# Staging the 64-bit words of one piece of weights in the place of the x of later chunks

## The chip, the core and the metric

The kernel runs on one core of one Trainium2 chip. The metric is the device time of one execution in microseconds (us). An execution ends when the last output row has been written to memory. The kernel before was timed three times: 731.48, 734.87 and 738.36 us, median 734.87 us.

## What is computed

Two stages follow one another. The first is a linear recurrence (RWKV-7) over 768 time steps with a 40x40 state for each of 4 batches and 8 heads. Its outputs, one row of 320 numbers for each of 3072 tokens, go through a feed-forward layer of width 2048.

```python
for t in range(S):                      # S = 768; state is (B, H, D, D) = (4, 8, 40, 40)
    y[:, :, t] = einsum('bhd,bhde->bhe', rt, state)
    Sa = einsum('bhde,bhe->bhd', state, at)
    state = state * wt[:, :, None, :] - einsum('bhd,bhe->bhde', Sa, bt) + einsum('bhd,bhe->bhde', vt, kt)
x = y.transpose(0, 2, 1, 3).reshape(3072, 320)
h = x @ w_in                            # 320 -> 2048
out = (h / (1 + exp(-1.702 * h))) @ w_out   # 2048 -> 320
```

The inputs are float32, but w_in and w_out are 64-bit floats. The kernel turns them into float32 on the chip.

## The kernel before

**Chunks and units.** Time is cut into 12 chunks of 64 steps. A chunk has two units (two batches each), so there are 24 units. `prep`, `inverse` and `solve` are the recurrence of one unit. `inverse` is a chain of five levels: a group of matmuls (`ps_level`), a subtraction on DVE (`E`, L686), a 32x32 transpose on DVE (`ES`, L648), a spreading to twice the size on POOL, DVE or ACT (`EX`, L653 and L655), and the next level. The copy `W` (L684) runs beside it. `solve` ends with the matmuls `ps_y`, with `zr` (L837) and with the product `x` (L847). `part_with` writes that x to memory (`x_dram`, L857), and `get_back` reads it back turned (`xT`, L861).

**The feed-forward layer.** `mlp(c)` takes the xT of both units of chunk c. `ps_up` multiplies by w_in in four groups (q = 0 to 3) of 40 matmul calls, ACT applies the gelu to each group (`g`, L882), and `ps_down` multiplies by w_out in two passes (p = 0 and 1) of eight parts (m = 0 to 7), eight matmul calls each. Each call of a float32 matmul appears as two matmuls in the trace. xT has three slots. Chunk c uses slot c mod 3, so chunk 0 uses slot 0, chunk 1 slot 1 and chunk 2 slot 2.

**The weights.** They come in eight pieces of 128x1280 64-bit words (1280 KB each). Pieces 0 to 3 are w_in, and `ps_up` group q needs piece q. Pieces 4 to 7 are w_out: parts m = 0 and 1 of `ps_down` need piece 4, parts 2 and 3 piece 5, parts 4 and 5 piece 6, and parts 6 and 7 piece 7. `weight(n, ...)` plans six steps for a piece: the transfer into a staging place (L433), one ACT instruction (`rebased`, L413), and five DVE instructions: L417, L421 and L422, L425, and L429 (`joined`). L429 writes the finished float32 words into `w_sb`. A staging place is twice the size of a finished piece. The list `raws` (L399) says where each piece is staged: a positive number is a position in the part of `w_sb` that is not yet filled, and -4 and -2 are the two halves of the buffer `extra`, called A and B here. In the kernel before, pieces 0, 4 and 6 use A one after the other, and pieces 3, 5 and 7 use B. Pieces 1 and 2 lie in `w_sb`. A transfer waits until the piece before it in the same place is joined (`before`, L407).

**What sets the order.** The class `Plan` writes the program out. Every step is a task with a rank, costs on the engines that may run it, and the tasks it needs. `order()` walks through time with these costs, and for each free engine takes the able task of the lowest rank. `paced()` repeats this in four rounds with release times for the feed-forward layer, and keeps the plan that ends first by its own costs. The tasks are then issued in that order, so each engine runs its instructions in a fixed order. The transfers are all issued by SP, in one order. A weight's rank is one of `RANKS` (L243: 14 to 41), a recurrence step's about 10 times its unit, and a feed-forward matmul's 10000 and more.

Of the kernel before, what the change touches and what calls it, by code (L numbers as in the profile page):

```python
# [21 lines left out]
INT64 = mybir.dt.int64  # L22
# [203 lines left out]
def rwkv7_gelu_quick(ctx: ExitStack, tc: tile.TileContext, time_d, v_d, w_d, wc_d, ak_d, b_d, rv_d, w_in, w_out, out):  # L226
    nc = tc.nc
    H, D, S = 8, 40, out.shape[0] // 4
    DM = H * D
# [3 lines left out]
    PIECE = w_in.shape[2]  # L233
    NF = w_in.shape[0] * PIECE // DM
    NM = NF // 2
    NK = DM // 64
# [17 lines left out]
    plan = Plan(dict(logw=3, wc=3, G=1, wch=3, wz=2, time=2, ak=2, b=2, rv=2, FT=3, GT=1, kh=2, bh=2, zr=2, rz=2,  # L254
                     A=1, B=1, RV=2, E0=2, W0=2, P21=2, W=2, E=2, ES=2, EX=2, T=2, Tc=1, QT=1, zraw=2, zT=1, M=2, x=1, xT=3, g=4, ob=1), 4)
    tiles, psums, drams = {}, {}, {}

    def single(name, shape):
        return const.tile(shape, FP32, tag=name, name=name)

    def buf(name, n, shape, dt=FP32):

        if (name, n) not in tiles:
            s = n % plan.slots[name]
            tiles[name, n] = work.tile(shape, dt, tag=f"{name}{s}", name=name)
        return tiles[name, n]
# [20 lines left out]
    def act(n):  # L287
        return {"ACT": 210.0 + 0.76 * n}
# [39 lines left out]
    for p in HALF:  # L328
        q = slice(p.start, p.start + MID)
# [59 lines left out]
    w_sb = single("w_sb", [128, NK * NM * 128 + NF * DM])  # L389
    w_in_sb = w_sb[:, :NK * NM * 128].rearrange("p (m k f) -> p m k f", m=NM, k=NK)  # L390
    w_out_sb = w_sb[:, NK * NM * 128:]

    extra = single("extra", [128, 4 * PIECE])


    most, least = (float(np.array(x, np.uint32).view(np.float32)) for x in (0x0FEFFFFF, 0x9FEFFFFF))


    raws = [-4, 4, 6, -2, -4, -2, -4, -2]  # L399

    def weight(n, rank, src):
        at = raws[n]
        raw = lambda: (w_sb[:, at * PIECE:(at + 2) * PIECE] if at > 0 else extra[:, (at + 4) * PIECE:(at + 6) * PIECE]).bitcast(INT64)

        scale = lambda: w_sb[:, n * PIECE:(n + 1) * PIECE].bitcast(INT32)

        before = [("weight", m) for m in range(n) if raws[m] == at]  # L407
        there = [("weight", m) for m in range(n) if raws[m] in (n, n - 1)]
        word = lambda dt, w: raw().bitcast(dt).rearrange("p (n two) -> p n two", two=2)[:, :, w]

        def rebased(t):

            nc.scalar.activation(scale().bitcast(FP32), word(FP32, 1), ACT.Prelu, scale=2.0 ** -112, alpha=2.0 ** 32)  # L413

        def bounded(t):

            nc.vector.tensor_scalar(scale().bitcast(FP32), scale().bitcast(FP32), least, most, ALU.max, ALU.min)  # L417

        def exponent(t):

            nc.vector.tensor_scalar(word(INT32, 1), scale(), 3, -2 ** 23, ALU.logical_shift_left, ALU.bitwise_and)  # L421
            nc.vector.tensor_single_scalar(scale(), scale(), 3, op=ALU.logical_shift_left)  # L422

        def fraction(t):
            nc.vector.scalar_tensor_tensor(word(FP32, 1), in0=word(UINT32, 0), scalar=2.0 ** -52, in1=word(FP32, 1),  # L425
                                           op0=ALU.mult, op1=ALU.mult)

        def joined(t):
            nc.vector.tensor_add(scale().bitcast(FP32), scale().bitcast(FP32), word(FP32, 1))  # L429

        one, two = 170.0 + 0.48 * PIECE, 150.0 + 1.05 * PIECE
        T = lambda *names: [(name, n) for name in names]
        plan.add(rank, {"SP": 350.0}, lambda t: nc.sync.dma_start(raw(), src), reads=before, writes=T("wt"), size=128 * PIECE * 8)  # L433
        plan.add(rank, act(PIECE), rebased, reads=T("wt") + there, writes=T("rebased"))
        plan.add(rank, {"DVE": one, "sbuf": True}, bounded, reads=T("rebased"), writes=T("bounded"))
        plan.add(rank, {"DVE": 2 * one, "sbuf": True}, exponent, reads=T("bounded"), writes=T("exponent"))
        plan.add(rank, {"DVE": two, "sbuf": True}, fraction, reads=T("exponent"), writes=T("fraction"))
        plan.add(rank, {"DVE": two, "sbuf": True}, joined, reads=T("fraction"), writes=T("weight"))

    def weights():  # L440
        for n in range(len(raws)):
            weight(n, RANKS[n], w_in[n] if n < NQ else w_out[n - NQ])
# [116 lines left out]
    at = lambda tiles, n: tiles[n % len(tiles)]  # L559
# [1 line left out]
    both = lambda i: zr_of(i)[:, :8 * 104].rearrange("p (j n) -> p j n", n=104)  # L561
    zraw_of = lambda i: buf("zraw", i, [128, 8, D])
    M_of = lambda i: buf("M", i, [128, 8, 104])
    xT_of = lambda c: buf("xT", c, [128, 2, NK, 128])
    kh_of, bh_of = lambda i: kh_t[i % 2], lambda i: bh_t[i % 2]
    zT_of = lambda i: zT_t[i % plan.slots["zT"]]

# [165 lines left out]
    def solve(i):  # L733
        c, p = divmod(i, 2)
        R = 20 * (i // 2) + 5 * (i % 2)
        T = lambda *names: [(n, i) for n in names]
        ahT = lambda: ak_of(i)[:, 0]

        if c > 0:
            plan.add(R, {"DVE": 490.0, "sbuf": True}, lambda t: nc.vector.tensor_mul(  # L740
                both(i)[:, :, 64:], zraw_of(i - 2), wz_of(i).unsqueeze(2).to_broadcast([128, 8, D])),
                     reads=[("zraw", i - 2), ("wz", i)], writes=T("zr"))
# [12 lines left out]
            def read_state(t):  # L755

                ps, rT = psum(t, "ps_rz"), rv_of(i)[:, 0]
                for u, b in product(BITS, BITS):
                    for f, e in QUARTERS:
# [5 lines left out]
                     reads=T("zT"), writes=T("rz"), pair=("rz", i))  # L765
# [94 lines left out]
            for h in HALF:  # L860
                nc.sync.dma_start(xT_of(c)[h, p].rearrange("q k n -> q (k n)"), drams[i].rearrange("(q k) n -> q (k n)", q=64))  # L861
        plan.add(-50, {"SP": 700.0}, part_with, reads=T("x"), writes=T("xd"), size=DM * 512)
        plan.add(-50, {"SP": 700.0}, get_back, reads=T("xd"), writes=[("xT", c), ("xs", (c, p))], size=2 * DM * 512)


    g_of = lambda n: buf("g", n, [128, 2, 2, 256])
# [60 lines left out]
    for i in range(NU):  # L927
        decay(i)
        if i + 3 < NU:
            load_w(i + 3)  # L930
        if i + 2 < NU:
            logarithm(i + 2)
        if i >= 2:
            load(i)
        prep(i)
        inverse(i)
        solve(i)
        if i % 2:
            mlp(i // 2)
# [88 lines left out]
```

## Time and profile before

| What | Value |
|---|---|
| median of three runs | 734.87 us |
| the profiled execution's own time | 741.96 us |
| its span, first to last instruction | 740.3 us |
| PE busy | 679.0 us (92%) |
| DVE busy | 445.9 us (60%) |
| ACT busy | 343.8 us (46%) |
| POOL busy | 214.5 us (29%) |
| mean granted TensorE clock | 0.959 |

PE is TensorE and PEld its loading of weights, DVE is VectorE, ACT is ScalarE, POOL is GpSimd, and SP the engine that issues the transfers. A line of a view of waits has the waiting engine and instruction, then `<-`, then what ended the wait, and then the total in us, the number of waits and the longest one. A line of a timeline has the start and the duration in us, the engine, the line of the code and the tiles (out `<-` in); a bracket at its end is the engine's idle time ahead of it and what ended that. A line of a table of windows has the stretch in us, the busy time of each engine with the number of its instructions, the granted clock of TensorE (1.00 is full), the busy share of the transfer engines and the GB/s that they moved.

### The profile page before, as it was taken

How to read it: one execution, taken by the hardware profiler on the slowest of the kernel's cores; microseconds unless marked ns; L12 is line 12 of the kernel's file. 1: busy time of each engine (PE TensorE's matmuls, PEld its weight loads, DVE VectorE, ACT ScalarE, POOL GpSimd, SP SyncE). 2: the span in 40 equal slices, each digit the busy share in tenths (PEclk: the TensorE clock that was granted, in tenths of full speed). 3: DMA queues.
4: the chain of work that ended last, by engine and by line, in shares of the span. 5: the costliest groups of instructions: out<-in, count | busy, mean ns of one | idle time of the engine just before them, and what ended most of it. 6: DMA issues, size and time to landing. Idle time of an engine off the chain costs nothing.

```text
span 740.3 us, 43272 instructions
## 1 busy us (share of the span) xinstructions
PE 679.0 (92%) x20096; PEld 560.7 (76%) x20096; DVE 445.9 (60%) x795; ACT 343.8 (46%) x666; POOL 214.5 (29%) x279
## 2 busy tenths in 40 slices
PE   4575895899999999999999999999999999999997
PEld 3465773687888977887887888988888798777564
DVE  5788798878558566666557467656666546542000
ACT  4555465445535535545645526445446345332120
POOL 7236124243323333322322233422441421200000
PEclk9576699899999999999999999999999999999999
DMA  7951544243251242341332233341331230110000
GB/s 227 350 177 53 168 139 148 65 117 107 57 169 47 77 122 73 87 136 49 99 102 71 74 95 104 98 120 55 99 101 50 83 93 4 40 48 29 13 9 19
DMA packets 31860, 69.80 MB, mean 94 GB/s; under 512 B 5056, under 2 KB 14272, under 8 KB 30656
## 3 DMA queue, kind: packets, MB, share of 16 engines
q1 hardware_dynamic: 31680, 67.03, 30.1%
q8 instruction: 158, 2.59, 1.5%
q14 instruction: 22, 0.18, 0.1%
HBM read 59.15 MB, written 7.86 MB: 91 GB/s over the span
## 4 chain that ended last, share of the span: by engine, by line
PE 77%; DVE 7%; ACT 5%; DMA 5%; issue 2%; POOL 2%; SPq 2%; DVEq 0%; POOLq 0%; ACTq 0%
PE ps_down L274 25%; PE ps_up L274 25%; PE ps_level L274 7%; PE ps_y L274 4%; PE ps_B L274 4%; PE ps_X L274 2%; PE ps_T L274 2%; PE ps_Q L274 2%; DMA ak<-in_ak 1%; PE ps_rz L274 1%; DVE ES L648 1%; PE ps_N L274 1%; PE ps_RV L274 1%; PE ps_A L274 1%; DMA extra<-in_w_out 1%
## 5 line engine op out<-in xcount | busy, mean ns | idle before, releaser
L274 PE MATMUL ps_up<-xT,w_sb 64*64 64x256 f32 x3840 | 251.3, 379 | 2.7 <-DVE RV L605 1.5
L274 PE MATMUL ps_down<-w_sb,g 64*64 64x320 f32 x3072 | 246.6, 436 | 4.9 <-DVE w_sb L429 2.5
L274 PEld LDWEIGHTS ps_up<-xT,w_sb 64*64 64x64 f32 x3840 | 152.7, 134 | 32.0 <-DVE RV L605 1.6
L274 PEld LDWEIGHTS ps_down<-w_sb,g 64*64 64x64 f32 x3072 | 135.6, 135 | 50.3 <-issue 7.6
L274 PEld LDWEIGHTS ps_level<-W,EX 64*64 64x64 f32 x3840 | 85.3, 141 | 41.6 <-ACT EX L653 14.3
L274 PE MATMUL ps_level<-W,EX 64*64 64x64 f32 (+1 forms) x3840 | 87.4, 226 | 26.6 <-ACT EX L653 11.6
L653 ACT ACTIVATE EX<-ES,quads 128x256 f32<-128x256 f32 x120 | 54.5, 501 | 59.7 <-DVE ES L648 57.5
L684 ACT COPY W<-ps_level 128x512 f32<-128x512 f32 x67 | 39.3, 586 | 71.5 <-PE ps_level L274 71.2
L882 ACT ACTIVATE g<-ps_up 128x1024 f32<-128x1024 f32 x48 | 49.1, 1024 | 42.5 <-PE ps_up L274 42.2
L686 DVE TENSOR_TENSOR E<-two,ps_level 128x256 f32<-128x256 f32 x96 | 39.7, 413 | 48.1 <-ACT W L684 48.0
L655 POOL TENSOR_TENSOR EX<-ES,quads 128x512 f32<-128x512 f32 x26 | 37.7, 1449 | 80.3 <-DVE ES L648 57.6
L648 DVE STREAM_TRANSPOSE ES<-E 128x256 f32<-128x256 f32 x120 | 53.2, 444 | 5.6
L582 POOL TENSOR_TENSOR kh<-time,G 128x320 f32<-128x320 f32 x22 | 19.7, 894 | 123.9 <-PE ps_y L274 72.1
L908 DVE TENSOR_TENSOR ob<-ob,ps_down 128x320 f32<-128x320 f32 x24 | 11.6, 485 | 63.4 <-ACT ob L906 63.0
L785 ACT COPY B<-ps_B 128x416 f32<-128x416 f32 x41 | 20.6, 507 | 62.4 <-PE ps_B L274 62.4
L847 POOL TENSOR_TENSOR x<-zr,FT 128x128 f32<-128x128 f32 x80 | 42.7, 563 | 5.4 <-DVE zr L837 3.4
L643 POOL TENSOR_TENSOR W<-two,E 128x256 f32<-128x256 f32 x22 | 16.1, 731 | 95.5 <-DVE E L637 95.5
L274 PE MATMUL ps_y<-M,bh 64*64 64x104 f32 x768 | 36.7, 253 | 0.6 <-issue 0.6
L274 PE MATMUL ps_y<-RV,kh 64*64 64x104 f32 x768 | 36.2, 254 | 0.3 <-DVE M L801 0.3
L574 POOL TENSOR_TENSOR ak<-ak,FT 128x512 f32<-128x512 f32 x18 | 26.9, 1496 | 26.2 <-DMA ak<-in_ak 20.9
L801 DVE TENSOR_TENSOR M<-ps_X,later 128x832 f32<-128x832 f32 x24 | 24.5, 1019 | 15.9 <-PE ps_X L274 15.9
L655 POOL TENSOR_TENSOR T<-ES,quads 128x512 f32<-128x512 f32 x10 | 12.8, 1278 | 71.1 <-DVE ES L648 66.4
(128 smaller groups left out, 1088.2 us busy)
## 6 DMA issues: line engine op xcount, KB each, us to landing
ak<-in_ak SPq DMA_DIRECT2D x48, 160.0 KB
time<-in_time SPq DMA_DIRECT2D x24, 320.0 KB
rv<-in_rv SPq DMA_DIRECT2D x48, 160.0 KB
xT<-x_dram SPq DMA_DIRECT2D x48, 160.0 KB
wc<-in_wc SPq DMA_DIRECT2D x20, 264.0 KB
extra<-in_w_out SPq DMA_DIRECT2D x4, 1280.0 KB
logw<-in_w SPq DMA_DIRECT2D x24, 160.0 KB
b<-in_b SPq DMA_DIRECT2D x48, 80.0 KB
```

Source lines behind the costliest of these rows:

```text
L274: nc.tensor.matmul(o, lhsT, rhs, start=start, stop=True, skip_group_check=True)
L574: plan.add(R, {"DVE": 690.0, "POOL": 1270.0, "sbuf": True}, lambda t: of(t.engine).tensor_mul(ahT(), ahT(), FT_of(i)), reads=T("ak", "FT") ...
L582: plan.add(R + 4, {"POOL": 870.0, "DVE": 490.0, "sbuf": True}, lambda t, n=n, dst=dst: of(t.engine).tensor_mul(dst(i)[:, :, :D], by_head(t ...
L648: plan.add(rank, dve(256), lambda t: nc.vector.transpose(ES(n), source(t)), writes=[key("ES", n, 6)], **reads)
L653: nc.scalar.activation(dst[:, :, h], ES(n), ACT.Copy, scale=quads[:, h, :1])
L655: of(t.engine).tensor_mul(dst, ES(n).unsqueeze(2).to_broadcast([128, 8, 2, 32]), quads.unsqueeze(1).to_broadcast([128, 8, 2, 32]))
L684: plan.add(rank, any2(512), lambda t: copy(t.engine)(tiles_of(W(n + 1)), blocks(psum(t, ""), 64)), writes=[key("W", n + 1, 5)], pair=pair)
L686: plan.add(rank, dve(256), lambda t: nc.vector.tensor_sub(tiles_of(E(n + 1)), every(two32, [128, 2, 4, 32]), blocks(psum(t, ""), 64)[:, :, ...
L785: plan.add(R, any2(416), lambda t: copy(t.engine)(dst(), psum(t, "")[:, :, :208]), writes=[("Bv", i)] if x and c > 0 else T("B"), pair=(na ...
L801: plan.add(R + 1, dve(832), lambda t: nc.vector.tensor_tensor(M_of(i).rearrange("p (j b) n -> p b j n", b=2), psum(t, "")[:, :, :416].rear ...
L847: of(t.engine).tensor_mul(x[:, b ^ u, b], both(i)[:, at, :64], FT_of(i)[:, at])
L882: plan.add(-45, act(1024), lambda t: nc.scalar.activation(g_of(c * NQ + q).rearrange("p m r n -> p r m n"), psum(t, "").rearrange("p r (m ...
```

## The change

Piece 4 gets a staging place of its own: slots 1 and 2 of xT, which together are exactly as large as one piece of 64-bit words and first hold x for chunks 1 and 2. Piece 5 then follows piece 0 in A (it followed piece 3 in B), piece 6 follows piece 3 in B (it followed piece 4 in A), and piece 7 follows piece 5, now in A. The three slots of xT become one tile, `xT_all`, so that two of them can be addressed as one place. The reading back of x for chunks 1 and 2 additionally waits until piece 4 is joined. No arithmetic is added or taken away. Below L393 the lines move down by six in the changed file; line numbers in the text are those of the kernel before.

```diff
     extra = single("extra", [128, 4 * PIECE])
+    xT_all = single("xT_all", [128, plan.slots["xT"], 2 * NK * 128])
...
-    raws = [-4, 4, 6, -2, -4, -2, -4, -2]
+    spots = {"a": (extra, 0), "b": (extra, 2), "w4": (w_sb, 4), "w6": (w_sb, 6)}
+    raws = ["a", "w4", "w6", "b", "x", "a", "b", "a"]

     def weight(n, rank, src):
         at = raws[n]
-        raw = lambda: (w_sb[:, at * PIECE:(at + 2) * PIECE] if at > 0 else extra[:, (at + 4) * PIECE:(at + 6) * PIECE]).bitcast(INT64)
+        def raw():
+            if at == "x":
+                return xT_all[:, 1:].rearrange("p s n -> p (s n)").bitcast(INT64)
+            tile, k = spots[at]
+            return tile[:, k * PIECE:(k + 2) * PIECE].bitcast(INT64)
...
         before = [("weight", m) for m in range(n) if raws[m] == at]
-        there = [("weight", m) for m in range(n) if raws[m] in (n, n - 1)]
+        there = [("weight", m) for m in range(n) if raws[m] in (f"w{n}", f"w{n - 1}")]
...
-    xT_of = lambda c: buf("xT", c, [128, 2, NK, 128])
+    xT_of = lambda c: xT_all[:, c % 3].rearrange("p (q k n) -> p q k n", q=2, n=128)
...
-        plan.add(-50, {"SP": 700.0}, get_back, reads=T("xd"), writes=[("xT", c), ("xs", (c, p))], size=2 * DM * 512)
+        plan.add(-50, {"SP": 700.0}, get_back, reads=T("xd") + ([("weight", raws.index("x"))] if c in (1, 2) else []), writes=[("xT", c), ("xs", (c, p))], size=2 * DM * 512)
```

## The prediction, made before the changed kernel was run

> **What bounds the kernel now.** I read the page first, then a table of windows, the chain of work that ended last, the waits between 105 and 150 us, and the timelines of SP, ACT, DVE and PE around them.
>
> ```profile
> PE   4575895899999999999999999999999999999997
> PEclk9576699899999999999999999999999999999999
> ```
>
> These slices of 18.5 us say that PE is full from about 170 us on and has holes before. (In the last slice the final eviction and store are left.) A table of windows puts numbers to it:
>
> ```profile
> 0.00:81.30 81.30, 46.81 (x1512) 42.16 (x1512) 61.48 (x99) 43.45 (x110) 37.06 (x69) 0.71 0.60 199
> 81.30:111.20 29.90, 28.82 (x811) 23.34 (x814) 25.32 (x36) 17.73 (x25) 7.13 (x7) 0.94 0.46 149
> 111.20:144.10 32.90, 21.99 (x646) 15.55 (x638) 27.38 (x39) 17.62 (x36) 9.49 (x8) 0.84 0.31 103
> 144.10:171.60 27.50, 25.37 (x768) 21.73 (x768) 21.13 (x37) 14.45 (x27) 14.00 (x16) 1.00 0.46 129
> 171.60:735.50 563.90, 556.03 (x16368) 457.89 (x16368) 310.08 (x587) 250.14 (x467) 146.82 (x181) 1.00 0.26 75
> ```
>
> From 171.6 to 735.5 PE is busy 556.0 of 563.9 us at full clock. A change in the order of weights can't shorten that, but whatever brings PE earlier to 171.6 moves the end with it. The hole nearest to the change is 111.2 to 144.1: 10.9 us idle, at a clock of 0.84, while DVE is busy 27.4 of 32.9. Its waits:
>
> ```profile
> ACT w_sb L413 <- DMA extra<-in_w_out: 7.0, 1, 7.0
> PE ps_level L274 <- ACT EX L653: 4.9, 2, 4.4
> PE ps_down L274 <- DVE w_sb L429: 2.5, 2, 2.3
> DVE w_sb L417 <- ACT w_sb L413: 1.9, 1, 1.9
> DVE E L686 <- ACT W L684: 1.4, 1, 1.4
> ```
>
> ACT sits 7.0 us in front of the rebasing of a piece whose words have not landed. Queued behind it are a gelu and the EX and W copies, so PE waits 4.4 us for EX and DVE 1.9 and 1.4. SP and the chain say which pieces these are:
>
> ```profile
> 81.25 0.35 SPq L433 DMA_DIRECT2D extra<-in_w_out  x1
> 107.66 0.42 SPq L433 DMA_DIRECT2D extra<-in_w_out  x1
> 112.50 0.35 SPq L433 DMA_DIRECT2D extra<-in_w_out  x1
> ```
>
> ```profile
> 107.66 8.34 DMA extra<-in_w_out
> ...
> 127.65 2.48 DVE extra L425
> 130.16 1.50 DVE w_sb L429
> ...
> 131.70 4.54 PE ps_down L274 x32
> ...
> 142.57 1.48 DVE w_sb L429
> ```
>
> These are pieces 5, 6 and 7; piece 4 was issued at 40.17. Piece 6 could not start until piece 4 had left A (joined at 103.8), landed at 116.0 and was joined at 131.7. Piece 7 was issued when piece 5 left B (112.48), and DVE reached it only behind piece 6: joined at 144.04, with parts 6 and 7 of ps_down from 144.09.
>
> [...] Piece 6 took 8.34, sharing the engines with piece 7. [...] L422 took 1.95 us at 122.70, beside a POOL product, and 0.83 usually. [...] Here 32 ps_down matmuls took 4.54 us at 131.70 after a wait and 2.33 at 111.19[...].
>
> **The change part by part.** The changed kernel's order on each engine is known from its build, its times are not. After 173 of 945 groups of matmuls (172.5 us before) both orders have put out the same work; up to there they differ.
>
> *Piece 4's transfer* is issued by SP directly after the `time` load of unit 2 (31.2 before), about 9 us earlier. The engines move 326 GB/s from 20 to 40 us, so it pushes what follows (logw, rv, b, ak, time, logw, piece 5) back by 1.31 MB / 326 = 4.0 us at most. The first users: the Ln of that logw at 44.95, which the new order puts behind two B copies and an EX (about 48), and the product with ak on POOL at 59.25, issued at 37.66. Both have over 10 us, so the cost is hidden. If the cover is gone it is 0 to 4 us; I take 0.5. SP itself may stand at the next-but-some issue until piece 4 lands, some 3 us, also before 45.
>
> *Piece 6* waits for piece 3 (joined at 81.2) instead of piece 4. SP has it behind the ak load of unit 4 (85.50 before), so it goes at 82 to 86 [...]. The new order has ACT rebase it between two gelus, near 95: the 7.0 us of ACT are gone, and with them 1.9 + 1.4 = 3.3 us of DVE idle.
>
> *Piece 7* waits for piece 5, joined near 111 to 112 again, because DVE has it behind the products of unit 4's ps_A (105.14 before). On SP it also stands behind a b load that waits for unit 4's ps_N (110.98 before). So its transfer starts near 112 as before, but alone: [...] ACT being free, rebasing at 119 to 121 instead of 122.13.
>
> *DVE to the join of piece 7.* This sets the end of the hole. Counted over both orders up to that instruction, DVE loses the four x products of unit 2 (3.86 us at 96.00, now POOL's; 1.41 at 51.92, undisturbed), two zT copies (0.95), a W copy (0.65), an addition to B (0.57), and a P and a W of L640 and L643 (0.83). It gains six Tc copies (0.54 for two: 1.62), a zraw (0.44) and a zr (0.66). Net 1.7 to 4.1 us less. With 3.3 us of idle gone, the join comes at 144.0 - 3.3 - (1.7 to 4.1) = 136.6 to 139.0. I take 137.5, as POOL has more to do and will hold DVE up. This is 6.5 earlier.
>
> *PE.* Between the first ps_down and parts 6 and 7 the new order has 16.5 us of matmuls at full clock (48 calls of down 7.0, seven levels 3.2, y 1.4, four B 1.4, the rest 3.5), with parts 2 to 5 spread between levels. So PE could be there at 111.2 + 0.5 + 16.5 = 128 and with some waits for EX at 132: it will wait for the join, now in one place. 0.92 us (an A and an RV of unit 5) then lie ahead of it instead of behind.
>
> *Reading back x for chunk 1* waits for piece 4's join, near 103. In the new order its x comes from POOL after the same zr, about 103 too, and chunk 1's ups start at 163.4: 55 us of cover, cost nothing. Addressing xT as one tile adds no instruction, and the waits in the build name no new engine for chunk 0's ups.
>
> Sum: -6.5 - 0.9 + 0.5 = -6.9, say -7 us. From the span of 740.3 this gives 733.3, and 735.0 from the execution's own 741.96. That execution lay 7.1 above the median of 734.87; the same step from the median gives 728.
>
> **Rivals.** *A, the forecast*: ACT's stop gone, DVE sets piece 7; 4 to 11 us saved, 724 to 731. Chance 0.48. *B, DVE eats it*: DVE has some 24 us of work from piece 5's join to piece 7's whatever ACT does, and its contention with POOL (about 1 us each on three instructions of the hole) may grow. Then the join comes at 141 to 143 and 0 to 4 us are saved: 731 to 735. For it speaks DVE's 27.4 of 32.9 us; against it the 3.3 us that are plainly ACT's. 0.22. *C, PE leads*: the levels run without holes and the clock stays up, PE reaches the end of the hole at 130 to 132: 13 us saved, 722. Against it stands the DVE sum. 0.08. *D, slower*: the planner has also reordered the recurrence against the feed-forward layer from about 345 us on. Before, 7.9 us of those 564 are idle. Each further per cent of idle costs 5.6 us, so at 15 us (2.7%) the gain is gone, and at 22 us it is slower by 7: 737 to 745. For it: ACT's table loads and SP's order sit on that stretch too; against it: DVE is only 55% busy there. 0.22, of which 0.16 lie over 1%. *That the change doesn't do what it says*: piece 7 still waits for piece 5. This is in B.
>
> **How the numbers follow.** 1% is 7.35 us, about what a measurement of this kernel can tell from none: under 727.5 is faster, over 742.2 slower. A lies a little less than two thirds above 727.5: 0.32 faster (with the measurement's spread), 0.16 same. B is all same, C all faster, D 0.16 slower and 0.06 same. So 0.40, 0.44 and 0.16. The range 720 to 739 holds A, B, most of C and the better part of D; A's own is 724 to 731.
>
> **What would show it.** ACT's wait for `extra` gone, with piece 6 issued near 85 (right) or after 100 (wrong). Piece 7 issued near 112 and joined near 137. PE's one long wait in the hole in front of parts 6 and 7, for L429. The group that starts at 172.5 then starts near 165. Waits for rv, ak or logw transfers before 75 us would show the cost of the early fetch. PE idle after that group of 8 us would leave D out, of 15 or more prove it. The forecast is wrong if the join comes by 133 or after 142.

## The result, and the profile after

The changed kernel took 729.88 us (median of 10 executions, 727.34 to 732.53), the kernel before in the same session 736.37 us (median of 10, 731.48 to 738.44): ratio 0.9921, 95% interval [0.9898, 0.9944]. Of 736.37 us that ratio takes off 5.8 us; the two medians, of which it is not the quotient, differ by 6.5. The forecast was 728.0 with a range of 720 to 739.

The profiled execution took 729.5 us (span 727.8). That is 12.5 us below the profiled execution of before (741.96), about twice what the medians show. Part of that belongs to the one execution of before: from its group at 172.5 us to its end it took 567.8 us, and the changed kernel takes 564.6 from the same group. e1b_places (below), which has the order of before, takes 564.7 there, with a span of 737.5. Against that one the changed kernel's span is 9.7 us shorter, and all of it lies ahead of the group.

The page of the changed kernel, the rows of PE and its granted clock in slices of 18.2 us:

```profile
PE   4565986999999999999999999999999999999997
PEclk9666998999999999999999999999999999999999
```

PE is full one slice earlier. The table of windows, cut at the same events as before: first `ps_up`, first `ps_down`, start of parts 6 and 7, the group up to which both orders have put out the same work:

```profile
80.00:111.50 31.50, 28.02 (x872) 23.07 (x872) 28.09 (x40) 17.27 (x29) 10.48 (x11) 1.00 0.40 135
111.50:138.70 27.20, 20.47 (x666) 15.59 (x670) 25.65 (x36) 16.28 (x38) 12.73 (x10) 0.87 0.29 94
138.70:163.20 24.50, 24.50 (x743) 22.41 (x737) 19.22 (x32) 14.45 (x29) 11.18 (x15) 1.00 0.49 148
163.20:723.00 559.80, 553.89 (x16356) 447.51 (x16352) 307.89 (x580) 248.78 (x472) 142.16 (x179) 1.00 0.26 75
```

At the first `ps_down` the two kernels are level (111.19 before, 111.57 after). Parts 6 and 7 start at 138.76 instead of 144.09, which is 5.3 us earlier, and the group starts at 163.18 instead of 172.53, 9.35 earlier. PE's idle time from the first `ps_down` to parts 6 and 7 is 6.7 us instead of 10.9, and none is left from there to the group (2.2 us before).

The transfers of pieces 4, 5, 6 and 7 in SP's timeline:

```profile
29.74 0.33 SPq L439 DMA_DIRECT2D xT_all<-in_w_out  x1
...
42.40 0.33 SPq L439 DMA_DIRECT2D extra<-in_w_out  x1
...
81.37 0.35 SPq L439 DMA_DIRECT2D extra<-in_w_out  x1
...
111.10 0.35 SPq L439 DMA_DIRECT2D extra<-in_w_out  x1
```

Piece 6 is issued at 81.4 instead of 107.7, piece 7 at 111.1. ACT rebases piece 6 at 90.94, and no wait of ACT for `extra` is left anywhere. The longest waits of PE and DVE from 104 to 140 us:

```profile
PE ps_Q L274 <- DVE T L661: 3.7, 1, 3.7
...
DVE E L692 <- ACT W L690: 2.6, 2, 2.1
...
PE ps_level L274 <- POOL EX L661: 1.4, 2, 0.8
PE ps_down L274 <- ACT g L888: 1.1, 1, 1.1
```

No long wait of PE for a join (L435) is among them. The longest one stands in front of `ps_Q`, a group of matmuls that needs `T`, which is what the last level of `inverse` gives, spread like an `EX`. DVE's timeline shows why (the rows between 122.31 and 135.80 that carry nothing here are left out):

```profile
117.45 0.78 DVE L423 TENSOR_SCALAR w_sb<-w_sb 128x1280 f32<-128x1280 f32 x1
118.27 1.78 DVE L427 TENSOR_SCALAR extra<-w_sb 128x1280 int32<-128x1280 int32 x1
120.09 1.93 DVE L428 TENSOR_SCALAR w_sb<-w_sb 128x1280 int32<-128x1280 int32 x1
...
122.62 1.07 DVE L661 TENSOR_TENSOR T<-ES,quads 128x512 f32<-128x512 f32 x1
...
135.80 2.02 DVE L435 TENSOR_TENSOR w_sb<-w_sb,extra 128x1280 f32<-128x1280 f32 x1
```

The first three are piece 6. They stand ahead of the `T` that `ps_Q` needs, and take 4.5 us, with POOL at work beside L427 and L428 (1.78 and 1.93 us; for piece 7, at 131.01 and 131.87 with POOL idle, they took 0.82 and 0.83). The last row is the join of piece 7, done at 137.82; the forecast was 137.5.

The next two lines have the whole stretch up to that join, first in the kernel before (to 144.04), then in the changed kernel (to 137.82). The engines stand in the order PE, PEld, DVE, ACT, POOL:

```profile
0.00:144.04 144.04, 97.61 (x2960) 81.05 (x2960) 114.13 (x172) 78.80 (x171) 53.62 (x84) 0.79 0.51 167
0.00:137.82 137.82, 92.61 (x2973) 77.62 (x2976) 114.00 (x170) 75.62 (x166) 61.06 (x91) 0.83 0.52 174
```

DVE is busy 114.13 us before and 114.00 after. So the join does not come earlier because DVE has less to do ahead of it. DVE's idle time fell, from 29.9 to 23.8 us.

### The profile page after: what moved, and what is told of

Same layout as the page of the kernel before. It is cut to its first block, busy times and chain, and to the rows that moved or that the text cites. A ratio compares the mean times of both kernels' runs of the same rounds, so it can differ in the third digit from the quotient of the medians.

```text
span 727.8 us, 43264 instructions
## 1 busy us (share of the span) xinstructions
PE 671.9 (92%) x20096; PEld 548.4 (75%) x20096; DVE 442.5 (61%) x782; ACT 339.8 (47%) x668; POOL 215.3 (30%) x284
## 3 DMA queue, kind: packets, MB, share of 16 engines
q8 instruction: 158, 2.59, 1.4%
## 4 chain that ended last, share of the span: by engine, by line
PE 83%; DVE 6%; ACT 4%; issue 3%; DMA 2%; POOL 1%; SPq 1%; DVEq 0%; ACTq 0%; POOLq 0%
PE ps_down L274 27%; PE ps_up L274 27%; PE ps_level L274 8%; PE ps_y L274 4%; PE ps_B L274 4%; PE ps_X L274 3%; PE ps_T L274 2%; PE ps_N L274 1%; PE ps_A L274 1%; PE ps_rz L274 1%; PE ps_Q L274 1%; PE ps_RV L274 1%; PE ps_zT L274 1%; DVE ES L654 1%; ACT g L888 1%
## 5 line engine op out<-in xcount | busy, mean ns | idle before, releaser
L274 PE MATMUL ps_up<-xT_all,w_sb 64*64 64x256 f32 x3840 | 247.8, 378 | 1.8 <-DVE B L794 0.9
L274 PE MATMUL ps_down<-w_sb,g 64*64 64x320 f32 x3072 | 240.6, 432 | 2.1 <-ACT g L888 1.1
L274 PEld LDWEIGHTS ps_up<-xT_all,w_sb 64*64 64x64 f32 x3840 | 152.3, 133 | 29.1 <-ACT g L888 1.1
L274 PEld LDWEIGHTS ps_down<-w_sb,g 64*64 64x64 f32 x3072 | 128.3, 134 | 49.4 <-issue 2.8
L659 ACT ACTIVATE EX<-ES,quads 128x256 f32<-128x256 f32 x112 | 50.8, 501 | 60.2 <-DVE ES L654 59.8
L588 POOL TENSOR_TENSOR kh<-time,G 128x320 f32<-128x320 f32 x22 | 21.6, 981 | 121.8 <-issue 70.7
L853 POOL TENSOR_TENSOR x<-zr,FT 128x128 f32<-128x128 f32 x84 | 46.4, 582 | 2.8 <-DVE zr L843 2.8
L661 POOL TENSOR_TENSOR EX<-ES,quads 128x512 f32<-128x512 f32 x23 | 33.8, 1471 | 44.6 <-DVE ES L654 31.2
L690 DVE COPY W<-ps_level 128x512 f32<-128x512 f32 x30 | 20.6, 688 | 24.1 <-PE ps_level L274 24.0
L807 DVE TENSOR_TENSOR M<-ps_X,later 128x832 f32<-128x832 f32 x24 | 24.4, 1018 | 14.8 <-PE ps_X L274 14.8
```

The costliest lines, as they stand in the source:

```text
L274: nc.tensor.matmul(o, lhsT, rhs, start=start, stop=True, skip_group_check=True)
L588: plan.add(R + 4, {"POOL": 870.0, "DVE": 490.0, "sbuf": True}, lambda t, n=n, dst=dst: of(t.engine).tensor_mul(dst(i)[:, :, :D], by_head(t ...
L659: nc.scalar.activation(dst[:, :, h], ES(n), ACT.Copy, scale=quads[:, h, :1])
L661: of(t.engine).tensor_mul(dst, ES(n).unsqueeze(2).to_broadcast([128, 8, 2, 32]), quads.unsqueeze(1).to_broadcast([128, 8, 2, 32]))
L690: plan.add(rank, any2(512), lambda t: copy(t.engine)(tiles_of(W(n + 1)), blocks(psum(t, ""), 64)), writes=[key("W", n + 1, 5)], pair=pair)
L807: plan.add(R + 1, dve(832), lambda t: nc.vector.tensor_tensor(M_of(i).rearrange("p (j b) n -> p b j n", b=2), psum(t, "")[:, :, :416].rear ...
```

## The experiments

All but e8_before_priced start from the changed file, so their lines are those of the changed kernel. They edit the list of tasks after the planner has made it, so that one thing moves and the rest of the order stays. Ratios are to the kernel before, run on the same chip in the same session. The join of piece 7 is from each kernel's profile, which is one execution; the two kernels with the order of before and its stop, before and e1b_places, differ there by 0.33 us.

| Kernel | Order | Join of piece 7 ends | Median us | Ratio, 95% interval |
|---|---|---|---|---|
| before | before | 144.04 | 735.4 to 737.5 | 1 |
| changed | changed | 137.82 | 729.88 | 0.9921 [0.9898, 0.9944] |
| e1b_places | before | 144.37 | 737.87 | 1.0008 [0.9992, 1.0024] |
| e2b_places_fetch | before | 142.51 | 737.39 | 1.0012 [0.9994, 1.0030] |
| e2c_places_fetch97 | before | 141.96 | 735.10 | 0.9989 [0.9973, 1.0004] |
| e5a_late_stop | changed, stop put back | 143.68 | 739.11 | 1.0025 [1.0006, 1.0044] |
| e5b_late_nostop | changed, transfer late | 138.14 | 730.23 | 0.9907 [0.9881, 0.9932] |
| e6_old_places | changed, old places | 137.07 | 729.32 | 0.9924 [0.9894, 0.9953] |
| e3_after_late6 | changed, piece 6 later on DVE | 137.36 | 732.51 | 0.9947 [0.9929, 0.9965] |
| e7_early_words6 | changed, piece 6 earlier on DVE | 138.13 | 728.38 | 0.9909 [0.9883, 0.9935] |
| e8_before_priced | a third one, old places | 148.72 | 742.57 | 1.0094 [1.0062, 1.0126] |

My theory was the forecast's: the early transfer of piece 6 ends ACT's stop of 7.0 us and DVE's waits behind it. The rival was that the planner's other order is the gain, whatever the places.

### The places alone, and the early transfer alone, with the order of before

In these kernels the planner still counts with the old places, so the order of before stays on every engine. e2 adds the early transfer, and e4 moves the four x products of unit 2 to POOL:

```diff
-        before = [("weight", m) for m in range(n) if raws[m] == at]
+        before = [("weight", m) for m in range(n) if old[m] == old[n]]   # old = [-4, 4, 6, -2, -4, -2, -4, -2]
...
-        plan.add(-50, {"SP": 700.0}, get_back, reads=T("xd") + ([("weight", raws.index("x"))] if c in (1, 2) else []), writes=[("xT", c), ("xs", (c, p))], size=2 * DM * 512)
+        plan.add(-50, {"SP": 700.0}, get_back, reads=T("xd"), writes=[("xT", c), ("xs", (c, p))], size=2 * DM * 512)
...
+    fetch = plan.made["wt", 6][0]                                        # e2 and e4
+    tasks.remove(fetch)
+    tasks.insert(tasks.index(plan.made["ak", 4][0]) + 1, fetch)
+    for t in plan.made["x", 2]:                                          # e4
+        t.engine = "POOL"
```

> The new places alone, with the order of the kernel before on every engine: piece 4 in the x slots, 5 and 7 in A, 6 in B, but the planner still counts with the old places, so piece 6's transfer keeps its late turn on SP, behind the logw issued at 107.2. Theory (an early transfer of piece 6 frees ACT and DVE): nothing is gained, since piece 6 is still issued at about 107 and lands near 116; ACT still stands some 7 us ahead of its rebasing, the join of piece 7 stays near 144 us, 735 to 738 us, ratio 0.998 to 1.003. Rival 1 (the gain is in the planner's other order, the places don't matter): the same. Rival 2 (the places themselves gain, by less sharing between transfers): ratio below 0.996.

> As e1_places, and only piece 6's transfer moved on SP, to directly behind the ak load of unit 4 (85.5 us before). All other engines keep the order of the kernel before. Theory: ACT's stop of 7.0 us goes (a new one of up to 3 us for piece 7's landing near 118 can come), the 1.9 and 1.4 us of DVE's waits go, the join of piece 7 comes at 139.5 to 141 instead of 144.0, and the end 3 to 4.5 us earlier: ratio 0.994 to 0.996. Rival 1 (the gain comes from the planner's other order): less than 1 us, ratio above 0.998, the join after 143 since DVE's work up to it is the same.

> As e2_places_fetch, and the four x products of unit 2 on POOL instead of DVE, at the same turn. DVE loses 3.86 us at 96 us (1.41 where it is undisturbed). Theory: those sit ahead of piece 4's join, so 1.4 us or so more at the join of piece 7 beyond e2_places_fetch, if DVE has no idle time to lose it in: ratio 0.001 to 0.003 below e2_places_fetch. If the time is lost again in DVE's wait for EX and W near 104 to 116 us: the same as e2_places_fetch within 0.001. Rival 1 (this is where most of the gain is): 3 us or more below e2_places_fetch.

The measured ratios are 1.0041 [1.0021, 1.0061], 1.0056 [1.0037, 1.0075] and 1.0039 [1.0019, 1.0059]. All three have a wait that no theory meant. In them the reading back of chunk 1's first x comes ahead of piece 4's join, in the same slots, so that a part of piece 4's words is lost and the join stands for the x:

```profile
DVE w_sb L435 <- DMA xT_all<-x_dram: 5.7, 1, 5.7
```

That line is from e1_places; in the other two it is 2.6 and 2.7 us. So they decide little on the theories. e4 differs from e2 by 0.0017, less than half the width of either interval, so in the order of before the x products are no large part of the gain. What they do show is what the changed kernel's added dependence (`get_back` waits for piece 4) prevents, and that a wait of DVE ahead of the joins comes out at the end: mended, the first two are 0.0033 and 0.0044, or 2.4 and 3.2 us, lower.

The next two put the reading back behind the join:

```diff
+    back = plan.made["xT", 1][0]
+    tasks.remove(back)
+    tasks.insert(tasks.index(plan.made["weight", 4][0]) + 1, back)
```

> e1_places mended: the reading back of chunk 1's first x is put out behind piece 4's join and no longer ahead of it (there DVE's join waited 5.7 us for it, and read x in place of weights). New places, the order of the kernel before on every engine, piece 6's transfer late. Theory (an early transfer of piece 6 frees ACT and DVE): no gain, piece 6 issued near 107, ACT's stop ahead of its rebasing 5 to 7 us, ratio 0.998 to 1.002. Rival 1 (the planner's other order gains): the same. Rival 2 (the places themselves gain, since piece 5 can be issued some 2 us earlier): below 0.996.

> e1b_places with only piece 6's transfer moved on SP to behind the ak load of unit 4. Theory: ACT's stop goes, and the join of piece 7 comes at 139.5 to 141.5; DVE is then without a gap of over 1 us from 104 to 136, since the 2.6 us that it stood for x in e2_places_fetch are gone; ratio 0.994 to 0.996, and 0.003 to 0.005 below e1b_places. Rival 1 (the gain is in the planner's other order): within 0.002 of e1b_places.

In e1b_places the ratio is 1.0008, piece 6 is issued at 106.6, ACT's stop is 7.2 us and the join of piece 7 ends at 144.37. The places alone do nothing that can be measured.

In e2b_places_fetch the ratio is 1.0012, which the theory had put at 0.994 to 0.996. The mechanism is there: ACT's stop is gone and the stretch from piece 4's join (105.66) to piece 7's (142.51) is 36.9 us instead of 40.9. But piece 4's join itself comes 2.2 us later. A row of PE's timeline says why:

```profile
93.25 0.25 PE L274 MATMUL ps_y<-RV,kh 64*64 64x104 f32 x1 [2.29 <-issue]
```

PE stands for 2.29 us in the middle of `ps_y`, for nothing that the profile names (the last section says where such stops fall). It begins at 90.96, and piece 6's transfer was issued at 85.81; e1b_places has no such stop there. So I moved the transfer away from that place:

```diff
-    tasks.insert(tasks.index(plan.made["ak", 4][0]) + 1, fetch)
+    tasks.insert(tasks.index(plan.made["xd", 2][0]), fetch)
```

> e2b_places_fetch with piece 6's transfer ahead of the x_dram of unit 2 (about 97 us) instead of at 85.8, where PE stood 2.3 us for nothing the profile names in the middle of ps_y while two pieces landed one after the other. All other engines keep the order of the kernel before. Theory (2.2 us of the gain were lost to that stop of PE): the stop at 91 goes, piece 4's join is back at 103.5, ACT still doesn't stand for piece 6, the join of piece 7 comes near 140.3 against 142.5 and the time 2 us or more below e2b_places_fetch: ratio 0.993 to 0.997. Rival (the order of the kernel before can't use an earlier piece 6 at all): within 0.0015 of e1b_places (1.0008).

The stop at 91 us is gone, piece 4's join ends at 104.18 and piece 7's at 141.96, 2.4 us before that of e1b_places. The ratio is 0.9989: 0.0019 below e1b_places, about 1.4 us, with intervals that overlap, and just outside the rival's 0.0015. The theory said 0.993 to 0.997, so it falls in its size: in the order of before, ending the stop is worth 2.4 us at the join and some 1.4 at the end, which these intervals cannot tell from nothing. It is not 7.

### The stop alone, within the changed order

Now the other way round: the changed order, with piece 6's transfer put back to a late turn. In e5a_late_stop the rebasing stands where ACT has to stop for it, in e5b_late_nostop where the words have just landed.

```diff
+    act = [t for t in tasks if t.engine == "ACT"]
+    turn6 = act[act.index(plan.made["rebased", 7][0]) - 7]               # e5b: - 2
+    for late, behind in (plan.made["wt", 6][0], plan.made["xT", 1][0]), (plan.made["rebased", 6][0], turn6):
+        tasks.remove(late)
+        tasks.insert(tasks.index(behind) + 1, late)
```

> The changed kernel, with piece 6's transfer put back to a late turn on SP (behind the reading back of chunk 1's first x, about 107 us; 81.4 in the changed kernel) and its rebasing on ACT put behind the W copy of 109.2, as in the kernel before: so ACT's stop comes back within the new order. Theory: ACT stands 5 to 7 us, W and EX behind it come later by as much, DVE reaches piece 7's join 4 to 6 us later (142 to 144) and the time is 4 to 6 us above the changed kernel: ratio to the kernel before 0.997 to 1.001. Rival 1 (the order on the other engines is the gain, the stop is hidden): within 1.5 us of the changed kernel, ratio 0.990 to 0.994.

> As e5a_late_stop, with the rebasing of piece 6 on ACT behind the W copy of 114.5 instead, where its words should just have landed. The transfer is as late as in the kernel before, and ACT stands for it 1 us at most. Theory in the form that it is ACT's stop that costs, not the late transfer itself: within 1.5 us of the changed kernel, ratio 0.990 to 0.994 (piece 7 lands 2 to 3 us later since both transfers overlap, and its rebasing can stand for it some 2 us). If the early transfer is needed for more than that: 0.995 or above.

e5a_late_stop lost the whole gain: ratio 1.0025, which is 0.0104 or 7.7 us above the changed kernel (4 to 6 were expected), and its join of piece 7 ends at 143.68. Its waits from 105 to 142 us:

```profile
PE ps_down L274 <- ACT g L888: 6.8, 1, 6.8
...
ACT w_sb L419 <- DMA extra<-in_w_out: 4.8, 1, 4.8
...
DVE E L643 <- ACT P L646: 4.4, 1, 4.4
```

A stop of 4.8 us on ACT holds a gelu and a `P` copy (from `ps_N`) behind it, and through them PE's first `ps_down` and DVE. e5b_late_nostop, whose transfer is just as late (106.54), has ratio 0.9907 and its join at 138.14. In its ACT timeline the two rebasings stand as follows:

```profile
114.75 1.42 ACT L419 ACTIVATE w_sb<-extra 128x1280 f32<-128x1280 f32 x1
...
119.41 1.39 ACT L419 ACTIVATE w_sb<-extra 128x1280 f32<-128x1280 f32 x1 [0.56 <-DMA extra<-in_w_out]
```

So what counts is that ACT's turn for piece 6 does not come ahead of its words, and not that they land early. The early transfer is not needed: DVE takes up piece 6 only at 117.5 in the changed order.

### The changed order with the old places

If the transfer of piece 6 can be late, the old places can carry the changed order too:

```diff
-        at = raws[n]
+        at, place = raws[n], ["a", "w4", "w6", "b", "a", "b", "a", "b"][n]
...
-            if at == "x":
-                return xT_all[:, 1:].rearrange("p s n -> p (s n)").bitcast(INT64)
-            tile, k = spots[at]
+            tile, k = spots[place]
...
+    places = [(one("wt", 4), one("wt", 5)), (one("wt", 5), one("wt", 6)), (one("wt", 6), one("xT", 1)),
+              (one("rebased", 5), one("rebased", 6)), (one("rebased", 6), turn6)]
+    for late, behind in places:          # one(key, n) = plan.made[key, n][0]; turn6 as in e5b_late_nostop
+        tasks.remove(late)
+        tasks.insert(tasks.index(behind) + 1, late)
```

> The order of the changed kernel on PE, DVE and POOL, but with the staging places of the kernel before (0, 4 and 6 in A, 3, 5 and 7 in B). Only transfers and rebasings are moved to where the old places allow them: piece 4's transfer takes the turn that piece 5's had (42.4), piece 5's that of piece 6 (81.4), piece 6's comes late, behind the reading back at 106; the rebasing of piece 5 takes piece 6's turn on ACT (90.9), and that of piece 6 stands behind the W copy of 114.5, as in e5b_late_nostop. Theory, as it stands after e5a_late_stop and e5b_late_nostop (the new order, with no stop of ACT in it, is the gain, and the places only led the planner to it): within 1.5 us of the changed kernel, ratio 0.989 to 0.993. Rival (the place in the x slots is needed, since one more piece is in flight early): 0.995 or above, with DVE or ACT waiting for piece 5 or 6.

The ratio is 0.9924 [0.9894, 0.9953], the span 726.8 and the join of piece 7 at 137.07: this is the gain of the changed kernel with the places of before. Its transfers of pieces 4 to 6 are within 1 us of those of the kernel before, and that of piece 7 is 2.7 us earlier:

```profile
40.72 0.33 SPq L439 DMA_DIRECT2D extra<-in_w_out  x1
...
80.35 0.35 SPq L439 DMA_DIRECT2D extra<-in_w_out  x1
...
107.79 0.55 SPq L439 DMA_DIRECT2D extra<-in_w_out  x1
...
109.77 0.35 SPq L439 DMA_DIRECT2D extra<-in_w_out  x1
```

This settles the main point. The new places are not what the chip gains from. They gave the planner other constraints, and the gain is the order that it then found, as long as ACT has no stop in it. Neither half gives the gain alone. Without the stop for piece 6 the order of before has a ratio of 0.9989 (e2c_places_fetch97), and with a stop of 4.8 us the changed order has 1.0025 (e5a_late_stop). Both together give 0.9907 to 0.9924.

### DVE's order ahead of ps_Q

The wait in front of `ps_Q` was the one that I had not foreseen. e3_after_late6 moves piece 6's three steps on DVE behind the `T`; e7_early_words6 moves them up into DVE's wait of 2.1 us at 102.4, which the early rebasing allows.

```diff
+    for step in ("exponent", "bounded"):                                 # e3
+        late = plan.made[step, 6][0]
+        tasks.remove(late)
+        tasks.insert(tasks.index(plan.made["T0", 3][0]) + 1, late)
...
+    early = plan.made["bounded", 6] + plan.made["exponent", 6]           # e7; dve = DVE's tasks in order
+    turn6 = dve[dve.index(plan.made["bounded", 5][0]) + 1]
+    for t in early:
+        tasks.remove(t)
+    tasks[tasks.index(turn6) + 1:tasks.index(turn6) + 1] = early
```

> The changed kernel with one thing moved: on DVE, piece 6's L423, L427 and L428 come behind the T of unit 3 (L661) instead of ahead of the ES, E and T that ps_Q needs. What the prediction had held (the join of piece 7 ends the hole): PE's wait of 3.7 us for T in front of ps_Q goes, but as much comes back in front of parts 6 and 7 for L435, and the time stays within 1 us of the changed kernel, ratio to the kernel before 0.991 to 0.993. Rival (DVE's order ahead of ps_Q is what holds PE): PE gains 2 to 3.5 us, 726 to 728 us, ratio 0.987 to 0.989, and the join of piece 7 isn't waited for.

> The changed kernel, with piece 6's L423, L427 and L428 on DVE moved up from 117.5 to directly behind the B of 101.8, where DVE stands 2.1 us for a W copy of ACT. This uses that piece 6 is rebased at 91 already. The three took 4.5 us at their old turn beside POOL. Expected if DVE's order ahead of ps_Q and the join of piece 7 are the bound of the hole: PE's 3.7 us in front of ps_Q go to 0.5 or less, the join of piece 7 comes at 134 to 136 instead of 137.8, and the time is 1.5 to 4 us below the changed kernel, ratio 0.985 to 0.990. If W and E at 104.5 then come later by up to 0.5 us and cost as much on PE's chain, or the wait only moves to the next EX: within 1 us of the changed kernel.

Neither gained what its theory had said. e3_after_late6 has ratio 0.9947, 1.9 us above the changed kernel, with intervals that overlap; PE's wait for `T` fell only to 2.6, PE still does not wait for L435, and 3.0 us for an `EX` of ACT came in its place. e7_early_words6 has ratio 0.9909: 0.0012 or 0.9 us below the changed kernel, which these intervals cannot tell from nothing; this is the second outcome that its text allows for. Its waits from 80 to 146 us:

```profile
DVE ES L654 <- ACT Tc L703: 2.7, 1, 2.7
...
PE ps_Q L274 <- DVE T L661: 2.6, 1, 2.6
```

With DVE free, its `ES` waits for ACT: the `Tc` (a copy of the last level's result) that it waits for stands on ACT behind a table load, four exponentials and the rebasing of piece 7 (118.81), and starts at 120.18. So in the changed kernel the wait in front of `ps_Q` had two causes of nearly the same length, and taking one away leaves the other.

### Another order with the old places

```diff
-        plan.add(rank, {"SP": 350.0}, lambda t: nc.sync.dma_start(raw(), src), reads=before, writes=T("wt"), size=128 * PIECE * 8)
+        plan.add(rank, {"SP": 350.0}, lambda t: nc.sync.dma_start(raw(), src), reads=before, writes=T("wt"), size=int(1.6 * 128 * PIECE * 8))
```

> The kernel before, old places and all, with one number changed for the planner: it prices the transfer of a piece of weights 1.6 times as large (the real transfer is unchanged). By its own price a piece landed 5.5 us after its issue; piece 6 took 8.3. So the planner makes another order, in which ACT's rebasing of piece 6 stands behind one gelu and one W more. Theory (the order without a stop is the gain, whatever the places): ACT's stop falls from 7.0 to 3 us or less, and the time to 728 to 733 us, ratio 0.990 to 0.997. Rival (the new places are what leads the planner to a good order, another order with the old places is no better): 0.998 or above, with a stop of ACT or DVE of 4 us or more still there between 100 and 145 us.

The theory in its simplest form falls here. ACT has no stop for `extra` at all, as hoped, and the kernel is the slowest of all: ratio 1.0094 [1.0062, 1.0126]. The rival's form of it (a stop of 4 us or more still there) is not what happened either. The planner now holds the steps of the weights back: piece 4 is joined at 109.57 instead of 103.77, so piece 6 is issued at 109.6, and piece 7 at 123.11 instead of 112.50:

```profile
146.76 1.96 DVE L429 TENSOR_TENSOR w_sb<-w_sb,extra 128x1280 f32<-128x1280 f32 x1
```

Its join of piece 7 ends at 148.72, 4.7 us later than before. No stop on ACT is not enough. Over the table the ratio goes with the join of piece 7: it is 0.991 to 0.995 where the join ends at 137 to 138 us, and 1.009 at 149. Between the changed kernel and this one 10.9 us of join go with 12.7 us of time (0.0173 of 736). But PE hardly waits for the joins (never in the changed kernel, 1.5 us in two waits in this one), so the join marks how far the work has come and is not shown to be what holds PE.

## Why the forecast held, point by point

**Piece 4's early transfer (0.5 us).** It is hidden at the first `ps_up`, which starts 1.3 us earlier than before (79.99 against 81.32). There is one cost that I had not named: PE stands 3.48 us at 48 us for nothing the profile names, in `ps_y`, beside piece 5's transfer (0.58 us before). It does not show in the time: e6_old_places, without the early transfer, has 1.36 us there, starts the first `ps_up` 1.0 us earlier (78.98), and takes as long. SP stood 2.8 us for piece 4's landing (some 3 foreseen).

**Piece 6 (issue 82 to 86, ACT's stop gone).** Right as a fact: issued at 81.37, rebased at 90.94, no stop. Wrong as the cause: e5b_late_nostop and e6_old_places have the late transfer and the gain, because there ACT's turn for it is late too. e5a_late_stop prices a badly placed turn at 7.7 us within the changed order, e2c_places_fetch97 its removal at 1.4 within that of before.

**Piece 7 and DVE's sum to its join.** Forecast 137.5, measured 137.82. Piece 7 was issued at 111.1 and rebased at 117.7, near the 112 and 119 to 121 foreseen. The 119 to 121 rested on an estimate of mine of how long a transfer takes alone. Measured, the rebasing came 6.6 us after the issue (111.10 to 117.71) with no wait of ACT in front of it; piece 6 of the kernel before, with piece 7 beside it from 112.50, took 8.34. That the sum came out right was in good part luck. The forecast took off 3.3 us of idle time of DVE and 3.2 us of work. The instructions that DVE loses and gains were counted rightly, but its busy time up to the join did not shrink: 114.13 us before, 112.59 in e1b_places, 114.00 in the changed kernel. POOL, which took the x products, is busy 61.06 us up to the join instead of 53.62, and some of DVE's other instructions took longer beside it (piece 6's L427 took 1.78 us, 0.80 before). So the term for the work was about 0 and not 3.2. In its place 6.1 us of DVE's idle time are gone, not 3.3: 4.0 behind the first `ps_down` and 2.1 ahead of it.

Nor do the two causes add up as the forecast had them. Against e1b_places (144.37) the join comes 2.4 us earlier when only the stop goes (e2c_places_fetch97), 0.7 when the order changes and a stop of 4.8 us stays (e5a_late_stop, whose profiled execution is one of its quickest), and 6.55 with both. Most of the gain needs the two together.

**PE "will wait for the join, now in one place".** This step failed. PE does not wait for L435 in front of parts 6 and 7. It waits 3.7 us earlier, in front of `ps_Q`, for a `T` that stands on DVE behind piece 6's words, and 2.8 us more in six shorter waits behind the first `ps_down`. When PE comes to parts 6 and 7 at 138.76, the join has been done for 0.9 us. It comes later than the 128 to 132 foreseen because it is busy for 20.5 us in the hole, at a clock of 0.87, instead of 16.5 at full clock, and stands for 6.7. In the kernel before, too, PE stood only 0.20 us for that join; the long waits there were for an `EX` (4.43) and for piece 6 (2.31). I had read the order of DVE for its sum only, not for what stands behind the weights in it. What sets the hole in its place is not isolated. From the first `ps_down` to the join DVE is busy 24.7 of 26.25 us, but e3_after_late6 and e7_early_words6 cut DVE's busy time up to the join by 2.0 us, to 111.97, and gain nothing that can be told from noise: their joins end at 137.36 and 138.13, and DVE now waits 2.6 and 2.7 us for ACT's `Tc`.

**The work behind the join (0.92 us).** This term was too small. From the start of parts 6 and 7 to the common group it was 28.4 us and is 24.4, so 4.0 us less. 2.2 of these are idle time of PE that the new order does not have (a wait of 1.46 us for DVE's `RV` at 171.6 is the largest; e1b_places has it too, 1.47), the rest is work that now lies ahead. So the sum in the profile is 9.35 us instead of the 6.9 worked out. The measured ratio gives 5.8, with an interval of 4.1 to 7.5, so at the level of the measured time the forecast of 7 stands.

**Get_back's added wait.** It cost nothing, as foreseen: piece 4 is joined at 100.8, and the reading back is issued at 105.96 because of the x itself. e1_places shows what it guards against.

**Rivals.** B (DVE eats it) predicted a join at 141 to 143: that is what the early transfer does in the order of before (141.96), but not in the changed one. Its reason holds, since DVE's work up to the join did not shrink; what it left out is that DVE's idle time could. C (PE leads) did not occur. D (the late part slower) did not either: from the common group to the end it is 564.6 us, against 564.7 in e1b_places.

**What stays open.** Three orders of this planner were measured with their own constraints: 736, 730 and 743 us. That is too few to say that the new places tend to give good orders; e6_old_places shows only that they are not needed for this one. The changed order differs from that of before on every engine, and which of these differences carry the gain was not tried, apart from the x products (e4_fetch_pool, in the order of before).

## What to carry to other kernels

Where a planner writes the order, a change of a buffer is above all a change of the order. Before the gain is put down to the buffer, run the new order with the old buffer and the old order with the new one. In an order that is fixed, a turn placed ahead of its data costs all that is queued behind it (4.8 us of ACT cost 7.7 of time here), and a late transfer with a late turn cost nothing (e5b_late_nostop). When reading an order for a forecast, read not only the sum ahead of the instruction that seems to set the end but also what each slow instruction stands in front of. And work that is moved to another engine is not yet time saved: here some of DVE's other instructions took longer beside POOL (L427 1.78 us against 0.82), and DVE's busy time up to the join stayed where it was (114.13 and 114.00 us).

## What the hardware showed that was not expected

PE stood for 2.29 us (e2b_places_fetch) and 3.48 us (changed kernel) in the middle of a run of short `ps_y` matmuls, with nothing named. The traces show where such stops fall. The page of the changed kernel lists a queue of the kind `instruction` with 158 packets:

```profile
q1 hardware_dynamic: 31680, 67.03, 29.8%
q8 instruction: 158, 2.59, 1.4%
```

2.59 MB in 158 packets are 16.4 KB each. The trace of the changed kernel records 40,435 instructions of PE, its semaphore instructions included, which are 256 to a packet. Over all 14 kernels of this document the timelines have 50 stops of PE of 0.5 us or more that are put down to "issue". Counted from the start of PE's instructions, every one of the 50 comes at the same place in a block of 256, to within four instructions. In every one PE goes on 1.25 to 1.57 us after the end of a packet of this queue; in the changed kernel that packet runs from 48.94 to 50.02, and PE goes on at 51.46. So these stops go with the packets of this queue; what the packets hold, and whether PE waits for it, is not shown.

Most packets go with no such stop: the changed kernel has two (4.5 us together) for 158 packets, e2b_places_fetch seven (7.8 us). Why these and not others is not shown. A transfer of 1.31 MB had been issued 5.6 and 5.2 us ahead of the two stops named above (at 42.40 in the changed kernel, at 85.81 in e2b_places_fetch), and in e2c_places_fetch97, where it came 12 us later (97.95), the stop at 91 us was gone.

DVE's L427 and L428 took 1.78 and 1.93 us beside POOL's products and 0.82 and 0.83 us with POOL idle (131.01 and 131.87), and the same three steps of piece 6 cost 4.5 us at 117 us in the changed kernel and 2.7 us at 103 us in e7_early_words6.
